# x of the next 512 tokens: one broadcasting transfer a chunk in place of two

## The chip, the core and the metric

The kernel runs on one core of a Trainium2 chip. The core has TensorE (PE; its weight loads are listed as PEld), VectorE (DVE), ScalarE (ACT), GpSimd (POOL), SyncE (SP, which here only issues transfers) and 16 DMA engines. The metric is the device time of one launch in microseconds; lower is better.

## The reference

```python
xn = layernorm(x)                                  # x: [1, 2048, 576]
q, k, v = split(xn @ wqkv)                         # 32 heads of 18
s = softmax(q @ k.T * 18 ** -0.5) @ v @ wo
gate, up = xn @ W_gate, xn @ W_up                  # 576 -> 4608 each
g = silu((relu(gate) * up) @ W_down)
out = x + s * g
```

All arithmetic is f32; the kernel keeps that precision by splitting each operand into a rounded high part and a low part and adding three products (high x high, high x low, low x high).

## The kernel before

The 2048 tokens are four groups of 512. The 576 features are nine chunks of 64. TensorE is used as two halves of 64 rows: in one step the upper half multiplies 64 features of x with W_gate and the lower half multiplies the same 64 features with W_up. So a chunk of x has to stand in SBUF twice, on partitions 0 to 63 and again on 64 to 127.

*First stretch, up to about 200 us.* Group by group the rows are normalised, turned to features by TensorE, split (tiles `x`), multiplied with wqkv (`pq`, `pv`), and q, k and v go to scratch tensors in HBM (`qd`, `kd`, `vd`; GpSimd issues these stores). `spill(g)` writes the split features of group g to the scratch `xTd[g]`, as 128 partitions x 1024 floats for each pair of chunks (512 high, 512 low). At the end of the work on group 2 the nine chunks of group 0 are read back by `load_x(0, c)`, and later the first strips of q and k (`kq`, `kA`) for the attention's first score matmuls (`pm`).

*Main stretch.* `units` are 144 pieces (group, tile of 128 of the 4608 hidden columns), 36 for each group, in order. `up(k)` computes gate and up of unit k (`pg`: nine chunks x three products x two halves), `down(k)` multiplies the hidden pieces of two units with W_down (`py`). The matmuls of attention are dealt into the steps of `up` by `emit_unit`: row maxima (`pm`) of one pair of heads and scores for exp (`psx`) of the pair before; the products with v (`po`) come after every odd unit.

*Where x is loaded.* Tiles `x` come from the pool `xA` of 11 buffers (`KC + 2`, `KC` = 9). Two buffers are free while a group runs, so in the last but one unit of a group `up` asks for chunks 0 and 1 of the next group. In the last unit, each time chunk c has been used for the last time, `up` asks for chunk c + 2 of the next group, which takes its buffer. The next unit reads all nine:

```python
if f == NF - 2 and k + 2 < len(units):
    for c in range(2):
        load_x(units[k + 2][0], c)
```

*What sets the order.* TensorE, VectorE and GpSimd run their instructions in the order of the program (`keep_in_program_order`). SP's transfers do so too until unit 17; after that only those wrapped in `pinned` (`load_x` is) and the rest are placed by the scheduler. Every SP transfer signals on one of eight semaphores (`DMAHW0` to `DMAHW7`, taken in turn), and waits until the earlier transfer of its semaphore has landed. I call these lanes; at most eight transfers of SP are under way.

*Other transfers named below.* `rg`: W_gate and W_up of a unit (288 KB each), split by GpSimd into `gw`; `rd`: W_down of a unit, split into `dw`; `kq`, `kA`, `qT`: strips of 18 rows of q and k, or 2 KB pieces with the row maxima (from `nr`); `od`: heads' output to scratch.

Of the kernel before, what the change touches and what calls it, by code (L numbers as in the profile page):

```python
# [9 lines left out]
F32 = mybir.dt.float32  # L10
# [9 lines left out]
def kernel(  # L20
# [10 lines left out]
    nc = tc.nc  # L31
    P = 128
    R = P // 2
# [39 lines left out]
    pinned = tc.keep_in_program_order  # L73
# [43 lines left out]
    xTd = dram.tile([NQ, XC, P, 2 * 512], F32, name="xTd")  # L117
# [43 lines left out]
    def xtile(pl):  # L161
        return pl.tile([P, 2, 512], F32R, tag="x", name="x")
# [136 lines left out]

    def load_x(g, c):  # L300
        xc = xtile(xA)
        for t in range(2):
            pinned(
                nc.sync.dma_start(
                    xc[t * R : (t + 1) * R].rearrange("p a s -> p (a s)").bitcast(F32),
                    xTd[g, c // 2, c % 2 * R : c % 2 * R + R],
                )
            )
        xcur.setdefault(g, []).append(xc)

    with ExitStack() as st:
# [295 lines left out]
        for g in range(NQ):  # L607
# [64 lines left out]
            else:  # L672
                for j in range(4):
                    v_job(wv, g, j)
                    if j == 0 and g == 0:
                        nxt = load_rows(g + 2)
                    if j == 1:
                        spill(g, marks[-1] if g == 0 else None)
                    if j and g == NQ - 2:
                        for c in range(3 * j - 3, 3 * j):  # L680
                            load_x(0, c)
# [24 lines left out]
    def up(k):  # L706

        g, f = units[k]
        gw = gus.pop(k)
        if k < N1 and (k % 2 == 0 or k == N1 - 1):  # L710
            ps = [psO.tile([P, 512], F32, name="po"), shared("pg2")]
        else:
            ps = [bank("pg0"), bank("pg1")]
        last = f == NF - 1 and k + 1 < len(units)
# [3 lines that stand above are left out]
        xg = xcur[g]  # L718

        def ops(t, c, i, j, rows):  # L720
            return gw[rows, i, c, :], xg[c][rows, j, :]

        def half(t):
            for n, _ in enumerate(row_half(ps[t], ops, t)):
                c = n // len(PRODUCTS)
                if t and last and n % len(PRODUCTS) == 2 and c + 2 < KC:
                    load_x(units[k + 1][0], c + 2)
                    if c == KC - 3:
                        load_up(k + 2)
                yield  # L730

        return ps, [half(t) for t in range(2)]
# [441 lines left out]
```

## Time and profile before

| | |
|---|---|
| median of 3 runs | 2575.8 us (2573.44 to 2575.84) |
| the profiled execution's own time | 2574.45 us |
| its span, first to last instruction | 2572.7 us |
| TensorE busy | 2565.1 us |
| VectorE, ScalarE, GpSimd busy | 1852.5, 1473.8, 1286.7 us |
| granted TensorE clock | 1.000 |
| DMA, mean over the span | 99 GB/s |
| transfers of `load_x` | 72 of 256 KB |

Busy times of different engines overlap. An engine that is busy for the whole span sets the time; another one matters where the first waits for it. In the lists below a row begins with the start in us from the span's start and the length, then engine, line, operation, names as out<-in, and a count. SPq and POOLq are the queues in which SP and GpSimd issue transfers: a row's length there is the time to issue, not to move the data. Rows of a window end with the granted clock, the mean busy share of the 16 DMA engines and GB/s.

### The profile page before, as it was taken

What the parts mean: (1) busy time and instruction counts of PE and PEld (TensorE: products, weight loads), DVE (VectorE), ACT (ScalarE), POOL (GpSimd) and SP (SyncE); (2) the same over time, 40 slices, a digit from 0 to 9 for tenths busy, and PEclk for the clock granted to TensorE, in tenths of its full rate; (3) what the DMA queues carried; (4) which work ended last, traced back from release to release, by engine and by line L of the source; (5) the groups of instructions that cost most, each with busy time, mean ns of one, the idle gap of its engine ahead of it and who ended that gap; (6) DMA issues with size and microseconds to landing.
All of it is one profiled execution on the core that took longest, in us unless ns stands there. A gap on an engine that the chain in (4) does not pass through costs nothing.

```text
span 2572.7 us, 61560 instructions
## 1 busy us (share of the span) xinstructions
PE 2565.1 (100%) x25301; PEld 2039.7 (79%) x25301; DVE 1852.5 (72%) x3019; ACT 1473.8 (57%) x3005; POOL 1286.7 (50%) x1035
## 2 busy tenths in 40 slices
PE   9999999999999999999999999999999999999999
PEld 8889997777777777777777777777777777777788
DVE  5336677777877788877777777887777877778136
ACT  3222146666666666666666666666666666666652
POOL 4246764444465444444465454444445445454554
PEclk9999999999999999999999999999999999999999
DMA  7864432333542223232353232322354332322246
GB/s 249 293 206 126 110 88 51 79 74 76 125 115 68 72 69 75 58 78 65 97 140 85 69 77 63 77 71 63 75 131 107 74 76 66 79 52 59 70 135 199
DMA packets 263833, 253.55 MB, mean 99 GB/s; under 512 B 27648, under 2 KB 208896, under 8 KB 263552
## 3 DMA queue, kind: packets, MB, share of 16 engines
q1 hardware_dynamic: 255808, 222.48, 34.2%
q0 software_dynamic: 7744, 27.14, 3.1%
q8 instruction: 199, 3.26, 0.5%
q14 instruction: 82, 0.67, 0.1%
HBM read 203.01 MB, written 46.01 MB: 97 GB/s over the span
## 4 chain that ended last, share of the span: by engine, by line
PE 98%; DVE 1%; POOL 0%; DMA 0%; issue 0%; ACT 0%; SPq 0%; POOLq 0%; ACTq 0%
PE pg L68 33%; PE po L68 18%; PE py L68 18%; PE pm L68 10%; PE psx L68 10%; PE pq L68 3%; PE pw L68 2%; PE pv L68 2%; PE tps L76 0%; DMA qd<-hh 0%; DMA xt<-in_A_x_dram 0%; POOL gw L85 0%; DVE hh L129 0%; DVE wqk L645 0%; DVE xn L374 0%
## 5 line engine op out<-in xcount | busy, mean ns | idle before, releaser
L273 DVE TENSOR_REDUCE mx<-pm 128x1 f32<-128x512 f32 x2048 | 1372.2, 690 | 355.2 <-PE pm L68 180.8
L68 PE MATMUL pg<-x,gw 64*128 64x512 f32 x7533 | 1359.2, 392 | 0.0
L97 ACT ACTIVATE p<-psx 128x512 f32<-128x512 f32 x2048 | 1097.2, 604 | 202.4 <-PE psx L68 161.7
L68 PEld LDWEIGHTS pg<-x,gw 64*128 64x128 f32 x7533 | 1028.9, 186 | 80.5 <-issue 1.9
L85 POOL TENSOR_TENSOR hh<-h,hh 128x512 fp32r<-128x512 f32 x144 | 185.8, 1290 | 802.5 <-ACT hh L747 798.7
L68 PE MATMUL py<-dw,hh 64*128 64x288 f32 x6912 | 478.1, 293 | 0.0
L68 PEld LDWEIGHTS py<-dw,hh 64*128 64x128 f32 x6912 | 472.8, 184 | 5.4 <-ACT h L97 0.6
L68 PE MATMUL po<-p,va 128*32 128x512 f32 x4096 | 452.7, 594 | 0.0
L68 PEld LDWEIGHTS po<-p,va 128*32 128x32 f32 x4096 | 126.5, 110 | 291.2 <-issue 280.0
L85 POOL TENSOR_TENSOR gw<-rg,gw 128x1152 fp32r<-128x1152 f32 x131 | 349.8, 2670 | 10.5
L797 DVE TENSOR_TENSOR y<-py,y 128x288 f32<-128x288 f32 x422 | 171.8, 453 | 139.3 <-PE py L68 139.2
L68 PE MATMUL psx<-qT,kq 56*128 56x512 f32 x608 | 231.1, 392 | 0.0
L68 PE MATMUL pm<-kq,qT 54*128 54x512 f32 x608 | 225.4, 395 | 0.0
L85 POOL TENSOR_TENSOR dw<-rd,dw 128x576 fp32r<-128x576 f32 x144 | 206.2, 1432 | 11.5
L68 PE MATMUL psx<-kq,kA 56*128 56x512 f32 x512 | 195.8, 393 | 0.0
L68 PE MATMUL psx<-kq 56*128 56x512 f32 x512 | 194.7, 392 | 0.0
L68 PE MATMUL pm<-kA,kq 54*128 54x512 f32 x512 | 191.5, 396 | 0.3 <-DVE mx L273 0.3
L68 PE MATMUL pm<-kq 54*128 54x512 f32 x512 | 191.1, 396 | 0.0
L781 ACT ACTIVATE mark<-ident 128x1 f32<-128x1 f32 x288 | 58.4, 203 | 218.3 <-PE py L68 218.2
L85 POOL TENSOR_TENSOR y<-add,y 128x576 f32<-128x576 f32 x61 | 87.3, 1432 | 187.4 <-ACT add L97 182.0
L85 POOL CAST gw<-rg 128x1152 fp32r<-128x1152 f32 x131 | 154.5, 1179 | 51.0 <-DMA rg<-in_B_W_up_dram 20.6
L747 ACT ACTIVATE hh<-h 128x512 fp32r<-128x512 f32 x144 | 90.7, 630 | 123.9 <-DVE h L740 123.9
(106 smaller groups left out, 2559.3 us busy)
## 6 DMA issues: line engine op xcount, KB each, us to landing
rd<-in_B_W_down_dram SPq DMA_DIRECT2D x144, 288.0 KB
rg<-in_B_W_gate_dram SPq DMA_DIRECT2D x131, 288.0 KB
rg<-in_B_W_up_dram SPq DMA_DIRECT2D x131, 288.0 KB
x<-xTd SPq DMA_DIRECT2D x72, 256.0 KB
qd<-hh POOLq DMA_DIRECT2D x16, 512.0 KB, 4.5
kd<-hh POOLq DMA_DIRECT2D x16, 512.0 KB, 5.8
xTd<-x SPq DMA_DIRECT2D x16, 512.0 KB
kq<-kd SPq DMA_DIRECT2D x210, 36.0 KB
```

Source lines behind the costliest of these rows:

```text
L68: return tc.keep_in_program_order(nc.tensor.matmul(*args, **kw))
L85: return lambda *args, **kw: tc.keep_in_program_order(op(*args, **kw))
L97: i = op(*args, **kw)
L273: vec(nc.vector.tensor_reduce(mx[:, h, b, j, c : c + 1], ps, axis=AX.X, op=ALU.max))
L747: copy = nc.scalar.activation(hhs[k][:, 0], h, AF.Copy)
L781: seen.append(pinned(nc.scalar.activation(mark, ident[:, :1], AF.Copy)))
L797: vec(nc.vector.tensor_tensor(ys[j][:, cs], outs_[m], ys[j][:, cs], ALU.add))
```

## The change

A chunk used to be loaded by two transfers of 64 rows x 4 KB, each from the same rows of `xTd`, one to the upper and one to the lower 64 partitions. Now one transfer writes all 128 partitions; its source pattern has a leading dimension of size 2 and step 0, so it reads the 64 rows twice.

```diff
     def load_x(g, c):
         xc = xtile(xA)
-        for t in range(2):
-            pinned(
-                nc.sync.dma_start(
-                    xc[t * R : (t + 1) * R].rearrange("p a s -> p (a s)").bitcast(F32),
-                    xTd[g, c // 2, c % 2 * R : c % 2 * R + R],
-                )
+        src = xTd[g, c // 2, c % 2 * R : c % 2 * R + R]
+        pinned(
+            nc.sync.dma_start(
+                xc.rearrange("p a s -> p (a s)").bitcast(F32), src.unsqueeze(0).to_broadcast([2, R, 1024])
             )
+        )
         xcur.setdefault(g, []).append(xc)
```

36 transfers are gone from SP (1,640 to 1,604); the other engines' instructions are the same in number. With fewer transfers the lanes fall otherwise, and the scheduler places some of SP's others at other points. On SP, at the first change of group (x of group 1; a row shows line, out<-in with buffer numbers, size and what it waits for), the last four chunks and what follows before:

```order
L304 DMA x_10310<-xTd_79 64x1024 [waits DMAHW1_49,PE_49]
L304 DMA x_10310<-xTd_79 64x1024 [waits DMAHW2_49]
L304 DMA x_10332<-xTd_79 64x1024 [waits DMAHW3_49,PE_49]
L304 DMA x_10332<-xTd_79 64x1024 [waits DMAHW4_49]
L304 DMA x_10349<-xTd_79 64x1024 [waits DMAHW5_49,PE_49]
L304 DMA x_10349<-xTd_79 64x1024 [waits DMAHW6_49]
L304 DMA x_10371<-xTd_79 64x1024 [waits DMAHW7_49,PE_49]
L304 DMA x_10371<-xTd_79 64x1024 [waits DMAHW0_49]
L97 DMA rg_10374<-in_B_W_gate_dram 64x9x128 [waits DMAHW1_49,Pool_49]
L97 DMA rg_10374<-in_B_W_up_dram 64x9x128 [waits DMAHW2_49]
L97 DMA rd_10458<-in_B_W_down_dram 128x576 [waits DMAHW3_49,Pool_49]
L97 DMA kq_2278<-qd_76 18x1024 [waits DMAHW4_49,PE_49]
```

and now all nine chunks:

```order
L304 DMA x_9929<-xTd_79 128x1x1024
L304 DMA x_9931<-xTd_79 128x1x1024 [waits DMAHW6_49]
L97 DMA rd_10216<-in_B_W_down_dram 128x576 [waits DMAHW7_49,Pool_49]
L304 DMA x_10237<-xTd_79 128x1x1024 [waits DMAHW0_49,PE_49]
L304 DMA x_10257<-xTd_79 128x1x1024 [waits DMAHW1_49,PE_49]
L97 DMA rg_10356<-in_B_W_gate_dram 64x9x128 [waits DMAHW2_49,Pool_49]
L304 DMA x_10278<-xTd_79 128x1x1024 [waits DMAHW3_49,PE_49]
L304 DMA x_10296<-xTd_79 128x1x1024 [waits DMAHW4_49,PE_49]
L304 DMA x_10317<-xTd_79 128x1x1024 [waits DMAHW5_49,PE_49]
L97 DMA rg_10356<-in_B_W_up_dram 64x9x128 [waits DMAHW6_49]
L304 DMA x_10333<-xTd_79 128x1x1024 [waits DMAHW7_49,PE_49]
L304 DMA x_10354<-xTd_79 128x1x1024 [waits DMAHW0_49,PE_49]
```

The two rg transfers (for unit 37, while unit 36 is the first to read the new x) stood behind all of x and now stand among its chunks, behind the fourth and the seventh; x takes nine turns of the lanes instead of eighteen.

On SP, at the start, the end of x of group 0 and what follows, before:

```order
L304 DMA x_2136<-xTd_79 64x1024 [waits DMAHW0_49,PE_49]
L304 DMA x_2136<-xTd_79 64x1024 [waits DMAHW1_49]
L97 DMA xTd_79<-x_1648 128x1024 [waits DMAHW2_49,DVE_49]
L97 DMA xTd_79<-x_1648 128x1024 [waits DMAHW3_49,DVE_49]
L97 DMA xTd_79<-x_1649 128x1024 [waits DMAHW4_49,DVE_49]
L97 DMA xTd_79<-x_1650 128x1024 [waits DMAHW5_49,DVE_49]
L97 DMA xTd_79<-x_1651 64x1024 [waits DMAHW6_49,DVE_49]
L97 DMA rg_2282<-in_B_W_gate_dram 64x9x128 [waits DMAHW7_49]
L97 DMA rg_2282<-in_B_W_up_dram 64x9x128 [waits DMAHW0_49]
L85 DMA kq_2278<-qd_76 18x1024 [waits DMASW4_49,DMASW3_49,DMASW5_49,DMASW2_49,DMASW6_49,DMASW1_49,DMASW7_49,DMASW0_49,DMAHW1_49,DVE_49,PE_49]
```

and now:

```order
L304 DMA x_2126<-xTd_79 128x1x1024 [waits DMAHW7_49,PE_49]
L304 DMA x_2128<-xTd_79 128x1x1024 [waits DMAHW0_49,PE_49]
L97 DMA xTd_79<-x_1648 128x1024 [waits DMAHW1_49,DVE_49]
L97 DMA xTd_79<-x_1648 128x1024 [waits DMAHW2_49,DVE_49]
L97 DMA xTd_79<-x_1649 128x1024 [waits DMAHW3_49,DVE_49]
L97 DMA xTd_79<-x_1650 128x1024 [waits DMAHW4_49,DVE_49]
L97 DMA xTd_79<-x_1651 64x1024 [waits DMAHW5_49,DVE_49]
L97 DMA rg_2273<-in_B_W_gate_dram 64x9x128 [waits DMAHW6_49]
L97 DMA rg_2273<-in_B_W_up_dram 64x9x128 [waits DMAHW7_49]
L85 DMA kq_2269<-qd_76 18x1024 [waits DMASW4_49,DMASW3_49,DMASW5_49,DMASW2_49,DMASW6_49,DMASW1_49,DMASW7_49,DMASW0_49,DMAHW0_49,DVE_49,PE_49]
```

The order is the same. The five xTd transfers and rg now take the lanes of the second to the eighth chunk, where before they took those of the sixth to the ninth; the first kq transfer has the lane of the ninth chunk as before.

## The prediction

> **What bounds the kernel now.** I read the page's busy times and its chain first, then TensorE's waits, then SP's list of transfers around the four places where x of a group is loaded.
>
> ```profile
> PE 2565.1 (100%) x25301; PEld 2039.7 (79%) x25301; DVE 1852.5 (72%) x3019; ACT 1473.8 (57%) x3005; POOL 1286.7 (50%) x1035
> PE 98%; DVE 1%; POOL 0%; DMA 0%; issue 0%; ACT 0%; SPq 0%; POOLq 0%; ACTq 0%
> PE pm L68 <- DVE mx L273: 0.3, 1, 0.3
> L304 SPq DMA_DIRECT2D x<-xTd x72: 444/584/1923, 81.7 to 1905.8; - x72
> ```
>
> TensorE is busy 2565.1 of 2572.7 us and holds 98% of the chain that ended last. The third row is its whole list of waits between 60 us and the end: 0.3 us. So all 72 x transfers, the first issued at 81.7 us, are hidden today. Whatever SP saves buys nothing, and the change can move the time only by making a transfer late enough for TensorE to wait. How much lateness is free is read from SP's and TensorE's lists around the change of group (start, length, what):
>
> ```profile
> 665.57 2.40 SPq L304 DMA_DIRECT2D x<-xTd  x4
> 682.74 10.18 SPq L304 DMA_DIRECT2D x<-xTd  x14
> 694.89 0.49 PE L68 MATMUL pg<-x,gw 64*128 64x512 f32 x1
> 704.99 6.61 PE L68 MATMUL py<-dw,hh 64*128 64x288 f32 x96
> 1271.60 2.40 SPq L304 DMA_DIRECT2D x<-xTd  x4
> 1301.72 0.49 PE L68 MATMUL pg<-x,gw 64*128 64x512 f32 x1
> 1878.48 3.09 SPq L304 DMA_DIRECT2D x<-xTd  x4
> 1908.62 0.49 PE L68 MATMUL pg<-x,gw 64*128 64x512 f32 x1
> ```
>
> Chunks 0 and 1 of group 1 are asked for at 665.57, the other seven from 682.74. The unit that reads them runs from 694.89 to 704.99, about 1.12 us a chunk, so the ninth is wanted at 694.89 + 8 x 1.12 = 703.87. From the first request to that need there are 38.3 us. The same sum gives 39.1 us at the two later changes (1271.60 to 1310.7, 1878.48 to 1917.6). All nine chunks have to come inside that cover.
>
> **What the edit does to the transfer itself.** Per chunk, two 256 KB transfers of 64 rows become one of 512 KB. The bytes are the same, and 36 issues of 0.584 us go away on SP (21 us of a queue that is not on the path): worth 0. The point that carries everything is on how many of the 16 DMA engines one transfer runs. The new source pattern is 2 (step 0) x 64 rows x 1024, against 128 partitions on the other side. Today's x transfers are 64 against 64. Does the trace show transfers whose outermost sizes differ or are small? It does:
>
> ```profile
> 710.98 4.49 SPq L97 DMA_DIRECT2D qT<-nr  x8
> DMA  0000000100000000010000001000000011000005
> DMA packets 78, 0.02 MB, mean 8 GB/s; under 512 B 72, under 2 KB 72, under 8 KB 78
> 715.57 2.16 SPq L97 DMA_DIRECT2D kA<-kd  x6
> DMA packets 110, 0.15 MB, mean 108 GB/s; under 512 B 36, under 2 KB 36, under 8 KB 110
> DMA packets 263833, 253.55 MB, mean 99 GB/s; under 512 B 27648, under 2 KB 208896, under 8 KB 263552
> ```
>
> The second and third rows are the window 714.0 to 716.6 us, in which four of the eight small nr transfers land (the four marks in the row of tenths). Each is 2 KB, 16 rows of 128 B on one side and 2 partitions on the other. Four of them bring 64 data packets, and the window has 72 packets under 512 B (the other 6 are the next transfer's), so two extra small packets a transfer. I read these as one end mark for each engine used: 2 engines, where the sizes are 16 and 2. The fifth row is the window 717.0 to 718.4, with transfers of 18 rows of 2 KB: 74 data packets, which is 4 transfers and 2 packets, and 36 small ones, so 9 each: 9 engines for 18 against 18. Taking for each transfer the largest number up to 16 that divides the outermost size of both sides, the program's 748 transfers of 64 or 128 rows use 16, the 704 of 18 rows use 9, the 256 of nr use 2: 11,968 + 6,336 + 512 = 18,816 marks. The rows of 128, 256 and 384 B that the program moves are 4,096 + 1,280 + 3,456 = 8,832 packets. Together 27,648, which is exactly the page's count of packets under 512 B. By the same reading the new transfer has 2 against 128 and runs on **2 engines**, 64 rows of 4 KB or 262,144 B on each; whether a 2 on the source side counts as it does on the destination side is the one thing that no row shows.
>
> The Trainium skill ("DMA: Bandwidth & Descriptors", section "Rules for kernel authors") says the same outright, that a leading zero-stride broadcast of c copies keeps the whole DMA on at most c engines; by it the sum below stands, and its 2-engine case is what the nr rows agree with. The same section also has a rule that speaks for the edit: two transfers to disjoint partition halves should be one 128-partition transfer, since both halves use all engines anyway; by that rule alone the time would be that of the first rival.
>
> **The price of two engines.** What one engine moves, from windows (the last two columns are the busy share of the 16 DMA engines and GB/s), and the stores' time to landing:
>
> ```profile
> 668.00:671.00 3.00, 3.00 (x28) 2.48 (x26) 2.71 (x4) 2.86 (x6) 0.00 (x0) 1.00 1.06 239
> 81.00:84.00 3.00, 3.00 (x28) 2.42 (x26) 0.17 (x1) 0.20 (x1) 0.00 (x0) 1.00 1.02 393
> 717.50:719.00 1.50, 1.50 (x16) 1.23 (x15) 1.16 (x3) 1.50 (x4) 1.50 (x1) 1.00 0.37 111
> qd<-hh POOLq DMA_DIRECT2D x16, 512.0 KB, 4.5
> ```
>
> x itself over 16 engines: 239 / (1.06 x 16) = 14.1 GB/s an engine. Spills and loads mixed at the start: 393 / (1.02 x 16) = 24.1. Small loads with most engines idle: 111 / (0.37 x 16) = 18.8, with gaps inside. The low 14.1 comes with 16 engines reading together; two engines ask for at most 48 GB/s, which the 393 row shows to be far from a shared limit. I take 24.1, so 262,144 B / 24.1 GB/s = 10.9 us a chunk, and keep 18.8 (13.9 us) inside the range and 14.1 (18.6 us) as a rival. If every transfer takes the same two engines (the marks cannot say which), nine chunks queue behind one another: 98 us. The fixed part, issue to landing, is 4.5 us for 512 KB less 512 KB / 393 GB/s = 1.3: about 3.1.
>
> *At each of the three changes of group.* 98 + 3.1, and about 3 us for the two rg and the rd transfer that the new order puts between the x transfers (288 KB each, 1/16 on each engine, at 14 to 24 GB/s about 1 us): 104.1 us from the first request to the last chunk. Less the cover of 38.3, 39.1 and 39.1: TensorE waits 65.8 + 65.0 + 65.0 = **196 us**, in steps of about 9.8 us a chunk. Behind the last x transfer stand rg and rd of the following units and q; SP gets to them as the earlier transfers of their lanes land, that is while TensorE waits anyway, and the rg of unit 37, the one after the unit that waits, is ahead of the eighth chunk. I cost them at nothing more; the cover is that same wait.
>
> *At the start.* x of group 0 is loaded from 81.69 and read by unit 0 from 199.7, a cover of 118 us. But SP's next transfers stand behind it:
>
> ```profile
> 81.69 33.11 SPq L304 DMA_DIRECT2D x<-xTd  x18
> q0 software_dynamic: 3711, 12.92, 40.7%
> 158.35 2.12 SPq L85 DMA_DIRECT2D kq<-qd  x6
> 165.60 2.26 SPq L85 DMA_DIRECT2D kA<-kd  x6
> 175.30 3.40 SPq L85 DMA_DIRECT2D kq<-kd  x6
> 184.92 0.39 PE L68 MATMUL pm<-kq 54*128 54x512 f32 x1
> 169.81 1.16 POOL L85 CAST gw<-rg 128x1152 fp32r<-128x1152 f32 x1
> ```
>
> The second row is GpSimd's queue between 83 and 180 us: 12.9 MB of stores, a sixteenth on each engine, sharing the two engines with x. Leaving out 1 MB that would be issued after POOL's cast at 169.81, which now waits for rg, it is 11.9 MB / 16 / 24.1 = 30.9 us. The ninth chunk lands at 81.7 + 3.1 + 98 + 30.9 = 213.7. The first kq transfer takes the lane of that chunk, so it moves from 158.35 to 213.7, 55.4 us. The pause of 5.1 us between the kq and kA rows goes, and of the 6.2 us between the end of the last kq issue (178.70) and the fourth score matmul (184.92) some 3.1 are spare. TensorE waits 55.4 - 5.1 - 3.1 = **47 us** at its first score matmuls. x of group 0 is there by then.
>
> **Sum.** 196 + 47 = 243 us, on the profiled execution's own 2574.45 us (1.75 above its span, and 1.35 below the median of 2575.8, which is the middle of three): 2817 us.
>
> **Rivals.** *Spread by destination rows.* If the 128 partitions decide, all 16 engines work, nine chunks take 4.7 MB / 239 GB/s = 20 us as now, and fit in the cover: 2574 us, not slower. For it: every transfer with 64 or 128 partitions in the trace uses 16. Against it: nr with its smaller size. It decides where nine chunks fit in 38.8 - 6.1 = 32.7 us, 3.6 a chunk, which at 24.1 GB/s takes six engines.
> *Two engines at the slow rate.* At 14.1 GB/s a chunk takes 18.6 us: 167.3 + 6.1 - 38.8 = 134.6, three times 404 us; at the start the ninth lands at 81.7 + 3.1 + 167.3 + 52.8 = 304.9, so 304.9 - 158.35 - 8.2 = 138 us: 3116 us. For it: it is the rate of this very read, 4 KB rows from the same scratch, and now both engines read the same rows. Against it: the other two rows.
> *Faster.* Fewer issues let SP run ahead. TensorE's idle time after 60 us is 0.3 us, so there is nothing to win: 2574 at best.
>
> **How the numbers follow.** Two engines at a rate from 18.8 to 24.1 GB/s: 0.80. The 18.8 end gives 3 x (125.5 + 6.1 - 38.8) = 278 and at the start 81.7 + 3.1 + 125.5 + 39.6 - 158.35 - 8.2 = 83, so 2936 us. The other end, if the fixed 6.1 us of each change and four fifths of the start's wait are hidden, is 196 - 18 + 10 = 188, so 2762. With a little beyond both, 2755 to 2960 holds about 0.80. The slow rate has 0.08, the spread over all engines 0.10, faster 0.02. A measurement of this kernel can tell about 0.2% (5 us) from no change: slower 0.88, same 0.10, faster 0.02.
>
> **What would show it.** Right: a DMA share near 0.13 (2 of 16) with some 48 GB/s for about 98 us from each first request; two marks a transfer on the page, so 36 x 2 in place of 72 x 16, 1,080 fewer packets under 512 B; TensorE idle of some 65 us at three places, before pg, released by x, and some 47 us before pm near 180; rows of pg, py and psx as long as before. Wrong: shares near 1.0 at 239 GB/s after 665 us, and no wait of TensorE. Stalls of 93 or of 135 us a change would say that the rate was mis-sized; a stall at the start far from 47 that the lanes and the stores were.

## The result, and the profile after

The changed kernel takes 2819.7 us (median of 5 runs, 2817.7 to 2821.4) against 2574.6 us before: a ratio of 1.095, interval 1.0935 to 1.0966. It is 245 us slower. The forecast was 2817 us.

The page of the changed kernel (busy times, end of the DMA lines, chain) answers to the rows shown of before:

```profile
span 2819.6 us, 61530 instructions
PE 2602.9 (92%) x25301; PEld 2047.6 (73%) x25301; DVE 1855.1 (66%) x3019; ACT 1475.5 (52%) x3005; POOL 1285.6 (46%) x1035
DMA packets 262753, 253.55 MB, mean 90 GB/s; under 512 B 26568, under 2 KB 207816, under 8 KB 262472
PE 87%; DMA 11%; SPq 0%; DVE 0%; POOL 0%; issue 0%; ACT 0%; POOLq 0%; ACTq 0%
```

TensorE is idle 216.7 us (2819.6 - 2602.9) where it was idle 7.6, and its busy time itself is 37.8 us longer with the same 25,301 matmuls; the two make up the 246.9 us by which the span grew. DMA now holds 11% of the chain. The packets under 512 B are 26,568, which is 1,080 fewer, the number forecast for 36 x 2 end marks in place of 72 x 16. The waits of TensorE by what it waited for (total, times, longest):

```profile
PE pg L68 <- DMA x<-xTd: 166.2, 21, 9.7
PE pm L68 <- DMA kA<-kd: 38.9, 1, 38.9
```

and the x transfers as SP's queue has them (time of one on SP, min, median, max in ns):

```profile
L304 SPq DMA_DIRECT2D x<-xTd x36: 489/5143/27088, 81.2 to 2132.0; - x36
```

There are twenty-one waits on x, seven at each change of group (chunks 3 to 9), and one long wait at the start on the first strips of k. One x transfer now holds SP for 5.1 us in the median and 27.1 at most, where it was 0.6 and 1.9. SP's and TensorE's lists around the first change, start and length:

```profile
714.06 1.14 SPq L304 DMA_DIRECT2D x<-xTd  x2
731.22 3.27 SPq L304 DMA_DIRECT2D x<-xTd  x2
743.32 0.49 PE L68 MATMUL pg<-x,gw 64*128 64x512 f32 x1
749.79 0.71 PE L68 MATMUL pg<-x,gw 64*128 64x512 f32 x2 [3.89 <-DMA x<-xTd]
759.92 0.79 PE L68 MATMUL pg<-x,gw 64*128 64x512 f32 x1 [7.72 <-DMA x<-xTd]
761.80 0.62 PE L68 MATMUL pg<-x,gw 64*128 64x512 f32 x1
...
815.82 1.22 PE L68 MATMUL pg<-x,gw 64*128 64x512 f32 x4 [9.43 <-DMA x<-xTd]
817.70 8.39 PE L68 MATMUL py<-dw,hh 64*128 64x288 f32 x95
```

The unit that reads the new x lasts from 743.32 to 817.70, 74.4 us where it lasted 10.1. Of these 64.3 us more, 55.0 are its seven waits on x and the rest is slower matmuls. From the first request (714.06) to the last chunk (815.82) are 101.8 us. From the third chunk to the ninth it is 66.0 us, 11.0 a chunk. What the DMA engines do in that time, in a window inside the wait, and TensorE's clock after it (the last three columns are granted clock, DMA share, GB/s):

```profile
756.00:776.00 20.00, 5.00 (x20) 3.00 (x20) 2.77 (x4) 2.39 (x4) 0.00 (x0) 0.50 0.13 50
817.70:826.00 8.30, 8.30 (x100) 8.30 (x98) 4.44 (x10) 1.82 (x6) 1.29 (x1) 0.77 0.31 90
```

A share of 0.13 is 2 of 16 engines, and 50 GB/s are 25 for each. By SP's list the fourth to the seventh chunk are under way in this window, and still no more than two engines are busy: all of them take the same two. The clock column was not foreseen: it falls to 0.50 while TensorE waits, and the single matmuls in the waits (759.92 and 761.80 above) take 0.62 to 0.79 us instead of 0.39.

At the start, SP's and POOL's lists and TensorE's first score matmul:

```profile
81.21 101.84 SPq L304 DMA_DIRECT2D x<-xTd  x9
199.92 5.74 SPq L97 DMA_DIRECT2D rg<-in_B_W_up_dram  x1
207.64 5.59 SPq L85 DMA_DIRECT2D kq<-qd  x6
215.54 1.14 POOL L85 CAST gw<-rg 128x1152 fp32r<-128x1152 f32 x1 [45.10 <-DMA rg<-in_B_W_up_dram]
218.05 0.76 PE L68 MATMUL pm<-kA,kq 54*128 54x512 f32 x1 [38.92 <-DMA kA<-kd]
```

The first kq transfer goes out at 207.6 instead of 158.35, POOL's cast waits 45 us for rg, TensorE waits 38.9 us, and unit 0 begins at 248.3 instead of 199.7: 48.6 us.

### The profile page after: what moved, and what is told of

It reads as the page before. It is cut to its first block, busy times and chain, and to the rows that moved or that the text cites. A ratio compares the mean times of both kernels' runs of the same rounds, so it can differ in the third digit from the quotient of the medians.

```text
span 2819.6 us, 61530 instructions
## 1 busy us (share of the span) xinstructions
PE 2602.9 (92%) x25301; PEld 2047.6 (73%) x25301; DVE 1855.1 (66%) x3019; ACT 1475.5 (52%) x3005; POOL 1285.6 (46%) x1035
## 2 busy tenths in 40 slices
DMA packets 262753, 253.55 MB, mean 90 GB/s; under 512 B 26568, under 2 KB 207816, under 8 KB 262472
## 4 chain that ended last, share of the span: by engine, by line
PE 87%; DMA 11%; SPq 0%; DVE 0%; POOL 0%; issue 0%; ACT 0%; POOLq 0%; ACTq 0%
PE pg L68 30%; PE py L68 16%; PE po L68 16%; DMA x<-xTd 10%; PE pm L68 9%; PE psx L68 9%; PE pq L68 3%; PE pw L68 2%; PE pv L68 2%; PE tps L76 0%; PE warm L76 0%; DMA kq<-qd 0%; SPq L85 0%; DMA kq<-kd 0%; DMA rg<-in_B_W_up_dram 0%; SPq L97 0%
## 5 line engine op out<-in xcount | busy, mean ns | idle before, releaser
L68 PE MATMUL pg<-x,gw 64*128 64x512 f32 x7533 | 1381.9, 397 | 166.2 <-DMA x<-xTd 166.2
L68 PE MATMUL pm<-kA,kq 54*128 54x512 f32 x512 | 196.3, 406 | 39.1 <-DMA kA<-kd 38.9
L68 PE MATMUL psx<-qT,kA 56*128 56x512 f32 x416 | 158.6, 399 | 0.0
```

Source lines behind the costliest of these rows:

```text
L68: return tc.keep_in_program_order(nc.tensor.matmul(*args, **kw))
```

## The experiments

The theory: the leading size of 2 in the source confines a transfer to 2 of the 16 DMA engines, always the same two, and nine such transfers exceed the time that was free. The rivals: the merging itself, the step of 0 (the same rows read twice), or SP's new order.

**One transfer a chunk without the leading 2** (`stored_twice`). The scratch holds each chunk twice (the spill of two chunks becomes four writes of 64 rows):

```diff
-                xc.rearrange("p a s -> p (a s)").bitcast(F32), src.unsqueeze(0).to_broadcast([2, R, 1024])
+                xc.rearrange("p a s -> p (a s)").bitcast(F32), xTd[g, c]   # 128 rows
```

> One transfer a chunk, but without the leading size of 2: the scratch holds each chunk's 64 rows twice (the spill writes them twice, 17 transfers a group in place of 5), so the load is 128 rows against 128. Theory (the source's leading 2 confines the transfer to 2 of 16 engines): nine chunks take 20 us again, inside the cover of 38 to 39 us, no wait of TensorE on x; 2575 us, within 5. Rival (one larger transfer, its single semaphore or SP's new order is at fault): about 2820 us, waits of 65 us at three places.

Measured 2597.0 us, a ratio of 1.0086 (1.0071 to 1.0101). TensorE waits nowhere on x; its list of waits of that kernel, longest first:

```profile
PE tps L76 <- DVE x L129: 7.2, 1, 7.2
PE pm L68 <- DMA kA<-kd: 4.2, 1, 4.2
PE pm L68 <- DVE hh L129: 3.4, 1, 3.4
```

The 65 us at the changes are gone, so the theory holds there. The 22 us left were not expected. They lie at the start: unit 0 begins at 223.1 us instead of 199.7, and ahead of it the doubled spill holds SP:

```profile
75.86 57.65 SPq L97 DMA_DIRECT2D xTd<-x  x34
146.16 34.80 SPq L97 DMA_DIRECT2D xTd<-x  x17
```

These 51 spills held SP for 92 us, waits included, and what stands behind them is late. **The same without the doubled spill** (`twice_main`): group 0 is loaded by two transfers as before, and the second copy for groups 1 to 3 is made in HBM during the units:

```diff
+        if 4 <= k < 31:
+            g_, c_ = divmod(k - 4, KC)
+            for t_ in range(2):   # 54 copies of 256 KB into xTw
+                pinned(nc.sync.dma_start(
+                    xTw[g_, c_, t_ * R : (t_ + 1) * R], xTd[g_ + 1, c_ // 2, c_ % 2 * R : c_ % 2 * R + R]))
```

> One transfer a chunk with 128 rows on both sides for groups 1 to 3: the second copy of x's rows is made in the scratch by 54 HBM-to-HBM transfers of 256 KB during units 4 to 30; group 0 is loaded by two transfers as before. The 22 us of the kernel that stored x twice all lay before 215 us, where its doubled spill held SP. Theory: without that, one transfer a chunk costs and brings nothing: 2575 us within 3. Rival (the larger transfer costs something at the changes after all, or the copies are in the way): over 2580 us.

Measured 2574.0 us, a ratio of 0.9997 (0.9989 to 1.0006): no difference. One transfer a chunk costs nothing and brings nothing when both sides have 128 rows. At the changes SP issues x and rg in the order of the changed kernel (rg behind the fourth and the seventh chunk), so neither the merging nor the new order is at fault there.

**The leading size alone** (`two_blocks`). The source is two blocks of different rows, so nothing is read twice:

```diff
-        src = xTd[g, c // 2, c % 2 * R : c % 2 * R + R]
+        o = min(c // 2, XC - 3)
+        src = xTd[g, o : o + 2, c % 2 * R : c % 2 * R + R]   # [2, 64, 1024], no step of 0
```

> The leading size is 2 but nothing is read twice: the two halves come from two different blocks of 64 rows, so the lower half of x holds the wrong chunk. Theory (the size of the outermost dimension counts, not its step of 0): 2 engines, 2820 us within 15. Rival (the step of 0, or both engines reading the same rows at a time, makes the read slow): 2575 us if the step decides, or waits well under 65 us a change if it was contention for the same rows.

Measured 2818.7 us (1.0949, 1.0933 to 1.0966), the time of the changed kernel. Its waits on x are the same too:

```profile
PE pg L68 <- DMA x<-xTd: 163.7, 21, 9.7
PE pm L68 <- DMA kA<-kd: 39.1, 1, 39.1
```

So neither the step of 0 nor reading the same rows is at fault. The outermost size of 2 is. The rule of the Trainium skill that the prediction weighed ("DMA: Bandwidth & Descriptors", "Rules for kernel authors") says this of an outermost dimension smaller than 16 in general, with the broadcast as its example, and this run agrees: 26,568 packets under 512 B, 2 marks for each of the 36.

**Four and eight engines** (`lead4`, `lead8`). The leading size becomes 4 or 8:

```diff
-        src = xTd[g, c // 2, c % 2 * R : c % 2 * R + R]
+        src = xTd[g, c // 2, c % 2 * R : c % 2 * R + P // 4]       # or P // 8
-   ... src.unsqueeze(0).to_broadcast([2, R, 1024])
+   ... src.unsqueeze(0).to_broadcast([4, P // 4, 1024])          # or [8, P // 8, 1024]
```

> The leading size is 4: the source is 32 rows read four times in place of 64 rows read twice, so half of x's values are the wrong rows; bytes, rows and order stay. Theory: 4 engines, 131,072 B on each, 5.45 us a chunk at 24.1 GB/s; 49 + 6.1 - 38.8 = 16 us of waits at each change, with matmuls at half clock about 18, and at the start nothing to 5; 2575 + 53 = 2628 us (2615 to 2642), 1,008 fewer small packets than before the change. Rival (any repeated source is slow, whatever its size): 2820 us. Rival (only a size of 2 is special): 2575 us.

> The leading size is 8: 16 rows read eight times (x's values are mostly the wrong rows). Theory: 8 engines, 2.7 us a chunk, 24.5 + 6.1 = 30.6 us, under the cover of 38.3: no wait, 2575 us within 5; the point at which it decides lies between 4 and 8 engines. Rival (any repeated source is slow): 2820 us.

Measured 2662.0 us (1.0334, 1.0317 to 1.0351) and 2612.3 us (1.0149, 1.0128 to 1.0171). The counts of packets are those of 36 x 4 and 36 x 8 marks (26,568 + 72 and + 216). The page's row with 4:

```profile
DMA packets 262825, 253.55 MB, mean 95 GB/s; under 512 B 26640, under 2 KB 207888, under 8 KB 262544
```

and with 8:

```profile
DMA packets 262969, 253.55 MB, mean 97 GB/s; under 512 B 26784, under 2 KB 208032, under 8 KB 262688
```

The number of engines follows the leading size exactly, and the loss falls from 245 to 87 to 38 us. But 53 and 0 were expected. One error is in the sum: it lets nine chunks follow one another from the first request. The waits on x with 4 engines, and the DMA engines' rate between 665 and 735 us in 40 slices:

```profile
PE pg L68 <- DMA x<-xTd: 61.1, 17, 5.8
GB/s 0 166 197 94 96 103 103 103 103 23 9 7 171 80 147 92 80 103 98 103 90 97 108 193 81 105 103 103 103 124 195 140 96 103 103 205 172 76 102 71
```

The first two chunks, asked for at 668.14, are done near 681, some 4 us before the others are asked for (685.44), and next to nothing moves (23, 9 and 7 GB/s) between 680.8 and 686.0. So the cover that counts is that of the last seven. With 2 engines the second chunk is still under way when the third is asked for, and the sum is right. TensorE's busy time rose as well, by 25.1 us (2590.2 against 2565.1), where the expectation had some 6. The second error, with 8 engines, is the rate. Two windows inside the loads of the kernel with 8:

```profile
669.00:672.00 3.00, 3.00 (x28) 2.58 (x26) 2.73 (x4) 2.83 (x6) 0.00 (x0) 1.00 0.54 142
692.00:702.00 10.00, 8.71 (x77) 4.79 (x67) 4.78 (x7) 4.96 (x9) 0.97 (x1) 1.00 0.61 130
```

142 / (0.54 x 16) = 16.4 and 130 / (0.61 x 16) = 13.3 GB/s an engine, not 24; with a share above 0.5 other transfers are in the windows too. Here the waits on x were 25.1 us in all, and the busy time of TensorE rose by another 21.2 (2586.3 against 2565.1). This profile is of the longest of the four runs (2606.7 to 2621.0 us).

**Eight engines, different rows** (`lead8_rows`). Is it the same 16 rows, read by eight engines at once?

```diff
+        rows = xTd[g].rearrange("c p s -> (c p) s")[: 8 * R].rearrange("(b r) s -> b r s", b=8)
+        src = rows[:, c % 4 * 16 : c % 4 * 16 + 16]               # 8 blocks, 256 KB apart
```

> The leading size is 8, with eight blocks of 16 different rows instead of the same 16 rows eight times (x holds wrong rows). With the same rows, 8 engines moved only some 120 to 130 GB/s at the changes, 15 an engine, where 4 engines kept 26 an engine, and the kernel lost 38 us. Theory (engines that read the same rows at the same time slow each other): with different rows 8 engines reach about 190 GB/s, the last chunk is 4 us late or less at each change, 2575 to 2590 us. Rival (8 engines slow down whatever they read): 2612 us again.

Measured 2605.2 us (1.0129, 1.0106 to 1.0152); the intervals of the two kernels overlap. Its windows at the same places:

```profile
669.00:672.00 3.00, 3.00 (x40) 2.87 (x38) 2.96 (x6) 1.70 (x4) 0.00 (x0) 1.00 0.51 150
692.00:702.00 10.00, 8.26 (x69) 5.02 (x61) 6.09 (x9) 6.15 (x11) 0.00 (x0) 1.00 0.53 158
```

18.4 and 18.6 GB/s an engine, a little above 16.4 and 13.3. Whether the rows are some of it is not shown, since the runs lie among one another (2601.0 to 2616.9 here) and the windows of `lead8` are from its longest. With different rows the kernel still loses 31 us, so the same rows are not all of it. Nor is it the number of engines alone: in `twice_main`, where a chunk is 128 rows that lie one behind the other and each is read once, 16 engines read at once during the first two chunks of group 1:

```profile
667.50:669.50 2.00, 2.00 (x22) 1.64 (x20) 1.88 (x3) 1.99 (x5) 0.00 (x0) 1.00 1.00 401
```

That is 401 / 16 = 25 GB/s an engine, as with two. The kernel before, whose two transfers of a chunk read the same 64 rows, had 14.1 at this place. Why eight engines, and the 16 of before, are slower each stays open; the blocks' distance of 256 KB in `lead8_rows` is one thing that was not varied.

**The start and the changes apart** (`start_only`, `changes_only`). `load_x` chooses by group:

```diff
+        if g == 0:      # in the other kernel: g > 0
             (the one broadcasting transfer)
+        else:
+            (the two transfers of before)
```

> Only x of group 0 is loaded by the one broadcasting transfer; groups 1 to 3 by two transfers as before. Theory (the waits add): the start's price alone, measured as the shift of unit 0 from 199.7 to 248.2 us, 48: 2575 + 48 = 2623 us. Rival (part of the start's loss is caught up later, or the changes cost more without it): off that by over 10 us.

> Only x of groups 1 to 3 is loaded by the broadcasting transfer; group 0 by two transfers as before. Theory: three waits of 66 us: 2575 + 198 = 2773 us, and unit 0 begins near 200 us. Rival as for the start alone: off that by over 10 us.

Measured 2624.6 us (1.0195, 1.0181 to 1.0209) and 2769.0 us (1.0756, 1.0741 to 1.0770), against 2575.0 before: 49.7 and 194.1 us. Together 243.8, where the whole change costs 244.7 against the same runs of before. The two losses add.

**TensorE kept busy in its waits** (`warm`). In the first unit of groups 1 to 3:

```diff
+                if t and k and f == 0 and n % len(PRODUCTS) == 2 and 0 < c < KC - 1:
+                    dum = shared("dum")
+                    for _ in range(64):
+                        tp(dum[:, :P], ident, ident)
```

> The changed kernel with 64 transposes of the identity (about 7.5 us of TensorE, results unused) ahead of each of the chunks 3 to 9 of the first unit of groups 1 to 3, where TensorE waits about 9 us. Theory: TensorE's granted clock falls to 0.50 in these waits, and the last chunk (1.88 in place of 1.12 us) and the py matmuls behind it (8.2 in place of 6.4 us) are longer for it, 2.5 us a change; kept busy, the clock stays near 1.0 and 7.6 us come back: 2812 us. Rival (the slow matmuls lie beside the transfers and cost nothing): 2820 us. If the transposes end later than the transfer lands, it is longer than 2820.

Measured 2814.5 us (2813.9 to 2815.8), against 2819.7 (2817.7 to 2821.4) without the transposes: 5.1 us less. No run of one lies among those of the other, but they were measured on different occasions and the two ratios' intervals (1.0916 to 1.0945 and 1.0935 to 1.0966) overlap, so the gain is likely and not certain. The mechanism itself is seen in TensorE's list, in the chunk that comes last and the py matmuls behind it:

```profile
816.85 0.73 PE L68 MATMUL pg<-x,gw 64*128 64x512 f32 x4 [0.78 <-DMA x<-xTd]
817.89 6.67 PE L68 MATMUL py<-dw,hh 64*128 64x288 f32 x95
```

and in a window over the waits:

```profile
747.00:815.00 68.00, 61.31 (x508) 55.58 (x505) 7.09 (x11) 7.91 (x14) 4.93 (x6) 0.97 0.22 72
```

The clock is 0.97, the last chunk takes 1.04 us instead of 1.88, py 6.67 instead of 8.39. That is 2.56 us at this change, 7.7 for three; 5.1 came back. In the changed kernel the first unit and its py hold 27.8 us of TensorE's work (743.32 to 826.09, less 55.0 of waits), and before it was 16.7 (694.89 to 711.60). So of 11.1 us that matmuls took longer at this change, about 8.5 lay beside the transfers and cost nothing.

The Trainium skill ("TensorE: Matmul & The Clock Gate", section "Part 1: The HAM clock gate") says that an idle TensorE gets half its clock and that some 3.4 us of activity bring the full one back. The granted 0.50 in the waits agrees, and the clock of 0.77 over the 8.3 us after the last one fits a return after about 4 us of steady work (3.8 us at 0.50 and the rest at 1.00 make 0.77).

**Issued by GpSimd** (`by_gpsimd`). Only the queue differs:

```diff
-            nc.sync.dma_start(
+            nc.gpsimd.dma_start(
```

> The same broadcasting transfer, issued by GpSimd in place of SP. Theory (the nine transfers queue behind one another because SP's always take the same two engines): if GpSimd's also run on the same two engines each time, waits of about 65 us stay at the three changes, 2770 us or more; if its transfers take turns over the engines, nine of them work beside one another, nine chunks take some 15 to 30 us, and the kernel comes back to 2575 to 2600 us, with what GpSimd loses by waiting for the buffers. The Trainium skill (DMA: Bandwidth & Descriptors, Why a DMA increments its semaphore by 16 and not by 1) says that GpSimd's take turns from a cursor, and SP's the lowest-numbered; no run so far shows it.

Measured 2707.0 us (1.0514, 1.0499 to 1.0528), between the two cases. GpSimd's and TensorE's lists at the first change:

```profile
692.00 1.65 POOL L304 DMA_DIRECT2D x<-xTd  x2
717.17 2.39 POOL L304 DMA_DIRECT2D x<-xTd  x3
738.48 0.80 PE L68 MATMUL pg<-x,gw 64*128 64x512 f32 x2 [12.06 <-DMA x<-xTd]
738.75 2.35 POOL L304 DMA_DIRECT2D x<-xTd  x3 [19.19 <-issue]
```

and the DMA engines between 690 and 760 us, in 40 slices (tenths busy, GB/s):

```profile
DMA  0089522222102206999864333210254333334011
GB/s 0 0 169 191 106 104 99 104 99 100 29 0 67 101 5 189 193 193 128 96 131 126 147 154 154 110 52 7 9 55 99 150 159 157 157 85 42 37 54 70
```

Behind the first two transfers about 2 tenths are busy and some 104 GB/s move, where SP's two together moved 50. So GpSimd's work beside one another, on different engines. But it sends only two or three at a time and then pauses (19.2 us that no row explains). Both long pauses at this change end 0.3 us after TensorE has got the chunk it waited for (738.75 after 738.48, 752.42 after 752.15), so it may be that GpSimd goes on only when the transfers before have landed; no run tests that. Three waits on x remain at each change, 29.0, 26.8 and 25.9 us in sum. The start is late too: there TensorE waits once for 25.7 us on `hh`, whose stores now stand behind the x transfers in GpSimd's list.

## Why the prediction was right

- *What bounds the kernel, and that the saving on SP is worth nothing:* right. The kernel with one transfer of 128 rows is within 0.1% of before.
- *Two engines, read from the end marks of nr and of the 18-row strips:* right, and the open point in it is settled. A 2 on the source side counts, whatever its step: `two_blocks` takes the same time, and the marks go 2, 4, 8 with the leading size.
- *10.9 us a chunk:* right. 11.0 was measured from the third chunk to the ninth with the rg transfers in between, and 25 GB/s an engine. The row of 24.1 was the nearest. The reason for setting the 14.1 aside, that it comes with 16 engines reading together, is not borne out: in `twice_main` 16 engines moved 25 each. The choice was right and its reason was not, so there was luck in it.
- *196 us at the changes:* 194.1 with `changes_only`. It is not all idle time as forecast: at the first change 55.0 us are waits and not 65, because the slower matmuls of a chunk fill part of the time until the next one lands. The chunks came some 2 us earlier than the sum had it (101.8 us from request to last chunk against 104.1), and what the sum left out, the half clock, cost about that: the chunk at the end and py took 2.6 us longer. That the two small errors cancelled was luck.
- *47 us at the start:* 49.7 with `start_only`. The place was right. The first kq transfer moved to 207.6, 6 us earlier than the sum's 213.7, and the matmuls after the wait then ran at half clock and waited for more strips: between the first score matmul and unit 0 are 30.2 us (218.05 to 248.3) where there were 20.2 (179.45 to 199.7). All waits in this stretch are 43.7 us (38.9 on kA, 2.9 on kq, 1.9 on `hh`) where 47 were forecast; the 3 us less went into the slower matmuls, and more.
- *"pg, py and psx as long as before":* wrong. They took 0.62 to 0.79 us between the waits. It was a step that the prediction costed at nothing without naming a cover.
- *"It decides at six engines":* wrong. Eight engines still cost 38 us. The step that failed is the cover of 38.8 us for all nine chunks, which holds only while the engines never run dry between the first two and the last seven, and the rate of 24.1, in whose place eight engines had between 13 and 19.
- *SP behind the x transfers:* the prediction let SP wait on lanes. The trace shows it held by the x transfers themselves: at the start 4 to 27 us each from the third on (nine in 101.84 us), at the first change 5 to 10 each from the fifth on. That is about the pace at which a chunk drains, so I infer that the two engines' queues were full; no run takes that apart from a lane. Behind that, the first kq transfer still waited 1.6 us for an x transfer, as the forecast had it.

## What to carry to other kernels

Before merging transfers, look at the outermost size of both access patterns: in these runs the number of DMA engines was the largest number up to 16 that divides both, and a leading repeat of 2 brought this load from 239 GB/s to 50. The count of packets under 512 B on the page shows it at once: one small packet for each engine that a transfer of SP used. And a load that is hidden is worth nothing when it gets cheaper, but has only so much room to get dearer; here that was 38 us at each change of group.

## What the runs showed that was not expected

- Eight engines reading at once moved 13 to 19 GB/s each, two and four moved 25 or so each (4 engines: 103 GB/s in the loads' steady slices, 50 for 2). It is due neither to reading the same rows alone nor to the number of engines alone: with 128 rows behind one another 16 engines moved 25 each.
- A transfer's time on SP is not fixed: 0.6 us in the median before, 5.1 and at most 27.1 with x on two engines, and TensorE's own list shows the price at the start, where kq, rg and kA stand behind x. While SP is held, every later transfer of its queue is late, whatever engines it would use.
- GpSimd's version of the transfer brought 32,760 more packets under 512 B (59,328 against 26,568), about 910 for each of the 36. What they are stays open.
